# The last chunk's second product as three float32r products of split operands

## The chip, the cores and the metric

The kernel runs on one NeuronCore of a Trainium2 chip. A core has five engines, each with its own in-order program: TensorE (PE in the profile; its weight loads are listed as PEld), VectorE (DVE), ScalarE (ACT), GpSimd (POOL) and SyncE (SP, which here only issues DMAs). TensorE reads SBUF and writes to PSUM; the other engines work on SBUF and PSUM, GpSimd on SBUF alone. The engines wait for one another through semaphores. The metric is the device time of one execution in microseconds (us).

## The reference

All data are float32. A recurrent cell (mLSTM) runs over S = 768 steps for 4 batches and 8 heads of size 40; its output, reordered to x with 3072 rows (batch x step) and 320 columns, goes through two matrix products with a sigmoid-approximated GELU between them:

```python
    m_new = np.maximum(f_gate[:, :, t] + m, i_gate[:, :, t])
    f_stab = np.exp(f_gate[:, :, t] + m - m_new)
    i_stab = np.exp(i_gate[:, :, t] - m_new)
    m = m_new
    C = f_stab[:, :, None, None] * C + i_stab[:, :, None, None] * np.einsum('bhd,bhe->bhde', vt, kt)
    n = f_stab[:, :, None] * n + i_stab[:, :, None] * kt
    h_tilde = np.einsum('bhde,bhe->bhd', C, qt)
    nq = np.einsum('bhd,bhd->bh', n, qt)[:, :, None]
    denom = np.maximum(np.abs(nq), 1.0)
    o = 1.0 / (1.0 + np.exp(-o_gate[:, :, t]))
    y[:, :, t] = o * h_tilde / denom
...
    h = x @ w_in
    g = h * (1.0 / (1.0 + np.exp(-1.702 * h)))
    return (g @ w_out).astype(np.float32)
```

Here `w_in` is 320 x 2048 and `w_out` 2048 x 320. The change is in `g @ w_out`.

## The kernel before

The 768 steps are cut into six chunks of 128 (`NW` = 6, chunk number `w`). One chunk holds 128 steps of all four batches, so the two products have 512 rows of x in a chunk: four row blocks `b` of 128. The main loop (line 980) does for each chunk `w`: the first product and GELU of chunk `w`; then the second product of chunk `w`, cut into blocks, with the attention of chunk `w + 1` put between these blocks. The program order of every engine is the order in which the Python code issues its instructions; nothing is reordered (`manual_schedule`). So "behind" on an engine means later in the code.

**First product** (`up_fast`, line 789, from chunk 1 on). The 2048 hidden columns are 16 blocks of 128, worked on in eight pairs `j`. Each operand is split into a high part with 12 bits (`x_high`, `w_high`: a ScalarE copy to float32r with scale `BIAS`) and what remains; a pair is 16 float32r matmuls with 512 columns into two `main` and two `side` banks of PSUM. Then ScalarE takes the side banks times -4096 into the tile `g` (L823), VectorE adds main times (1 + 1/4096) to it (L825), and one pair later ScalarE applies the GELU in place (L784, `gelu_fast`). Even pairs take their banks from `banks()`, two tiles of two banks used in turn; odd pairs take single banks from the pool `ps_m`. So a pair uses the banks of the pair two before it.

**Second product, chunks 1 to 5** (`down_fast`, line 876). `w_out` stays in SBUF as `w_out_sb`, 16 blocks `f` of 128 rows by 320 columns. It is seen as four quarters, `w00`, `w01`, `w10`, `w11` (blocks 0-7 or 8-15, columns 0-159 or 160-319). Two row blocks at a time are multiplied with it by a seven-product scheme (Strassen-Winograd): seven products of 8 float32 matmuls with 160 columns (L889), on `g` or on sums of `g` (`s`), and on a quarter or on sums of quarters (`t1`, `t2`, `t4` in `t_sb`). The sums of weights are made once, in chunks 0 and 1, by GpSimd (L848); one of them, `weight_sums(2)`, overwrites `w01` with `w11 - w01` in chunk 1. The sums of `g` are made by GpSimd (`hidden_difference` L857, `hidden_sums` L865, L868) beside the pairs and by VectorE (L865, L868, `last_sums` L874) at their end. Each product is added from PSUM into an output tile by VectorE (L892, L894); a finished row block of 128 x 320 is stored by SP (L898). A chunk has 14 such blocks; list index `i` in the loop of line 1066.

**Between the blocks of chunk `w`** stands the attention of chunk `w + 1` (`attention`, line 967): exponentials on ScalarE, masks and decays on GpSimd, scores and values on TensorE, the output's scaling on VectorE. Its result goes to DRAM and back as squares (`seam_out` L587, `seam_in` L596), is transposed on VectorE (`seam_turn`, L603) and split (`split_x` L765, L766 on ScalarE; `split_on` L773, L775, L778 on VectorE) for the next chunk's first pair. SP also brings in `w_diff` and `w_low` from DRAM again for the next chunk (L754, L750), issued at `i` = 11 and 13.

**Chunk 0** takes its second product directly (`down`, L835: 320 columns in float32, 64 matmuls), and converts the weights on the way in.

SBUF tiles come from pools; a tile with the same tag in the same pool takes the room of an older one and waits until that one's last reader is done. The tiles that this change reuses are `v_st`, `k_st`, `k_sq`, `q_sq`, `t_sb`, `state0` and `state1` (inputs and states of the attention), the buffers of `kT`, `qT` and `wt` (attention), of `w_high` and `w_low` (tag `wb`) and of `w_diff` (pool `sp`, tag `g`).

Of the kernel before, what the change touches and what calls it, by code (L numbers as in the profile page):

```python
# [18 lines left out]
L = 128  # L19
# [12 lines left out]
def kernel(  # L32
# [44 lines left out]


    f_sb, i_sb = {}, {}
    k_st = const.tile([L, BH * D + DP - D], FP, name="k_st")  # L80
    q_sq = const.tile([L, BH // 2 * 4 * D + 32], FP, name="q_sq")
    k_sq = const.tile([L, BH // 2 * 4 * D + 32], FP, name="k_sq")
    t_sb = const.tile([128, 3, NH * DH], FP, name="t_sb")
# [4 lines left out]
    v_st = const.tile([L, BH, D1], FP, name="v_st")  # L88
# [4 lines left out]
    w_out_sb = const.tile([128, NF, DM], FP, name="w_out_sb")  # L93

    def load_gates(w):
        for dst, src in ((f_sb, f_gate), (i_sb, i_gate)):
# [43 lines left out]
    w_out_flat = w_out_sb.rearrange("p f m -> p (f m)")  # L140


    def piece_in(c, n):
# [7 lines left out]
    def piece_out(n):  # L151
        parts, c = [], n * 512
        while c < n * 512 + 512:
            f, m = divmod(c, DM)
            e = min(c + DM - m, n * 512 + 512)
            parts += [(slice(0, 128), slice(c - n * 512, e - n * 512), out_bits[:, f, 2 * m:2 * (m + e - c)])]
            c = e
        return w_out_flat[:, n * 512:(n + 1) * 512], parts

    pieces = []  # L160
    for n in range(4):
# [67 lines left out]
        G.memset(t[:, :, D:DP], 0.0)  # L229

    mark = const.tile([L, 1], FP, name="mark")
    state = [const.tile([128, BH // 2, D1], FP, name=f"state{i}") for i in range(2)]
    state_mid = const.tile([128, BH // 2, D1], FP, name="state_mid")

    m_at, ends = {0: m0}, {}
# [385 lines left out]
    def wait_for(x):  # L621

        G.tensor_copy(out=mark[0:x.shape[0]], in_=x[:, 0:1])
# [206 lines left out]
    def down(w, b, n):  # L830
        if n == 0:
            o_ps[w, b] = ps_m.tile([128, DM], FP, tag="m", name="p_out")
        po = o_ps[w, b]
        for f in range(n * 4, n * 4 + 4):
            T.matmul(po, gs[w, f // 2][:, f % 2, b * L:(b + 1) * L], w_out_sb[:, f, :], start=(f == 0),  # L835
                     stop=(f == NF - 1))
# [6 lines left out]
    w00, w01 = w_out_sb[:, 0:NH, 0:DH], w_out_sb[:, 0:NH, DH:DM]  # L843
    w10, w11 = w_out_sb[:, NH:NF, 0:DH], w_out_sb[:, NH:NF, DH:DM]

    def weight_sums(n):
        out, a, b = ((t1, w01, w00), (t2, w11, t1), (w01, w11, w01), (t4, w10, t2))[n]
# [28 lines left out]
    def down_fast(w, c):  # L876
# [19 lines left out]
        def store(two):  # L896
# [8 lines left out]
                lambda: (product(block(1, 1), t4, (o10, o10)), store(1)),  # L905
                lambda: (product(total(2), w11, (o01, o01)), store(0))]


    def run(calls):
        for f, *args in calls:  # L910
            f(*args)
# [68 lines left out]
    for w in range(NW):  # L980
        more = w + 1 < NW
        if w == 0:
            for j in range(NF // 2):
                if j % 2 == 0:
                    ahead, behind = converted[j // 2]
                    if j:
                        run([(convert, p) for p in ahead])
                    run([(fetch, p) for p in fetched.get(j // 2, ())])
                    up(w, j, lambda: run([(columns_turn, 1) if p is None else (convert, p) for p in behind]), last_seam)
                if j == 6:  # L990
                    load(1, "o")
                if j == 1:
                    wait_for(w_in[1][:, 1, :])
                    scale(0, 1)
                    load(1, "v")
                if j < B and j % 2:
                    carry(0, j // 2)
                if j == 3:
                    masks()
                    gates(1)  # L1000
                    columns_in(1)
                if j == 4:
                    spread(1)
                    load_squares(1, "q")
                if j >= B:
                    transposes(1, j - B)
        else:
            if w == 1:
                split_diff(1)
                split_low(1, V)  # L1010
                more_rooms(1)
            for j in range(NF // 2):
                up_fast(w, j)
                if more and j == 0:
                    gates(w + 1)
# [33 lines left out]
                lag = 3 if w == 1 else 2  # L1049
                if lag <= j < 4 + lag:  # L1050
                    hidden_difference(w, j - lag)
                if j >= 6:
                    hidden_sums(w, (j - 6,), G)
            gelu_fast(w, NF // 2 - 1)
            if more:
                load(w + 1, "o")
            hidden_sums(w, (2, 3), V)
        side = attention(w + 1) if more else {}
        if more:
            rooms(w + 1)  # L1060
        if w == 0:

            blocks = [(lambda b=b, n=n: down(w, b, n)) for n0 in (0, 2) for b in range(B) for n in (n0, n0 + 1)]
        else:
            blocks = down_fast(w, 0) + down_fast(w, 1)
        for i, block in enumerate(blocks):
            if w == 0 and i == 0:
                columns(1)
                convert_begin(17)
                weights_exp(1, 0)  # L1070
                fill_squares(q_sq)
                convert_end(17)
                for n in (1, 3, 5, 7):
                    block_transposes(1, n)
# [12 lines left out]
            if w == 0 and i == 5:  # L1087
                wait_for(w_out_flat[:, 9 * 512:])
                weight_sums(1)
                weight_sums(3)  # L1090
            if w == 0 and i == 5:
                split_high(0)
                split_rest()
                split_high(1)
            if w == 0 and i == 9:
                split_diff(0)
                split_low(0, V)
                split_rest_low()
            if w and more:
                if i == 11:  # L1100
# [38 lines left out]
```

## Time and profile before

| what | value |
|---|---|
| median of three runs | 446.97 us (446.6 to 446.97) |
| the profiled execution | 447.5 us, its span 445.8 us, 12211 instructions |
| eight pairs of chunk 5 (last) | 382.91 to 412.29 |
| second product of chunk 5 | 412.29 to 442.73 |
| TensorE clock granted | 1.00 in every stretch asked for |
| DMA, all queues | 60.06 MB, mean 135 GB/s |

How to read it: times inside the span count from its start. A group line gives line number, engine, operation, tiles written and read, shape and count, then busy time and mean duration in ns, then the engine's idle time before it and what ended it. A timeline line gives start, length, engine, line, operation and count, with the idle time before it in square brackets. A line of the chain gives start, length and what the end waited for there. TensorE overlaps its matmuls, so the mean duration of one is longer than the distance from one to the next; a float32 matmul is recorded as two instructions and a float32r one as one. The form shows f32 for float32r operands of a matmul. Stretches list busy time and count for PE, PEld, DVE, ACT and POOL, then the granted clock, the DMA share and GB/s.

### The profile page before, as it was taken

How to read it: one execution, taken by the hardware profiler on the slowest of the kernel's cores; microseconds unless marked ns; L12 is line 12 of the kernel's file. 1: busy time of each engine (PE TensorE's matmuls, PEld its weight loads, DVE VectorE, ACT ScalarE, POOL GpSimd, SP SyncE). 2: the span in 40 equal slices, each digit the busy share in tenths (PEclk: the TensorE clock that was granted, in tenths of full speed). 3: DMA queues.
4: the chain of work that ended last, by engine and by line, in shares of the span. 5: the costliest groups of instructions: out<-in, count | busy, mean ns of one | idle time of the engine just before them, and what ended most of it. 6: DMA issues, size and time to landing. Idle time of an engine off the chain costs nothing.

```text
span 445.8 us, 12211 instructions
## 1 busy us (share of the span) xinstructions
PE 440.1 (99%) x4999; PEld 384.0 (86%) x4999; DVE 327.3 (73%) x660; ACT 228.9 (51%) x494; POOL 130.8 (29%) x131
## 2 busy tenths in 40 slices
PE   8999999999999999999999999999999999999997
PEld 6867887776889999888999888999888999888997
DVE  4888999989999877778686779686769566634512
ACT  5677779902787701687701486800486900366000
POOL 6401327440066700135700034700035610035000
PEclk9999999999999999999999999999999999999999
DMA  8999999017777427979026978216988306600000
GB/s 168 196 283 165 242 271 216 2 35 196 183 200 161 63 63 218 267 111 168 13 59 188 270 102 176 44 34 143 328 114 156 61 19 151 232 31 0 1 31 29
DMA packets 129656, 60.06 MB, mean 135 GB/s; under 512 B 102096, under 2 KB 122528, under 8 KB 129600
## 3 DMA queue, kind: packets, MB, share of 16 engines
q1 hardware_dynamic: 120512, 54.86, 55.8%
q10 hardware_dynamic: 8768, 4.28, 3.3%
q8 instruction: 39, 0.64, 0.6%
q0 software_dynamic: 320, 0.15, 0.2%
q14 instruction: 17, 0.14, 0.1%
HBM read 49.10 MB, written 10.16 MB: 133 GB/s over the span
## 4 chain that ended last, share of the span: by engine, by line
PE 93%; SPq 4%; DMA 2%; DVE 1%; issue 0%; ACT 0%; DVEq 0%
PE p_out L889 34%; PE p L806 17%; PE p_h L806 16%; PE p_out L835 8%; PE p_h L657 7%; SPq L132 3%; PE p L534 2%; PE p L490 2%; PE p L542 2%; PE p L633 2%; PE p_h L666 2%; DMA bits<-in_moe_w_in_dram 2%; DVE state L610 0%; PE p L406 0%; DVE state_mid L642 0%
## 5 line engine op out<-in xcount | busy, mean ns | idle before, releaser
L857 POOL TENSOR_TENSOR g<-g 128x512 f32<-128x512 f32 x20 | 25.8, 1297 | 159.5 <-ACT g L784 159.5
L889 PE MATMUL p_out<-w_out_sb,g 128*128 128x160 f32 x480 | 68.9, 300 | 0.0
L889 PEld LDWEIGHTS p_out<-w_out_sb,g 128*128 128x128 f32 x480 | 66.4, 190 | 0.6
L765 ACT ACTIVATE x_high<-xT 128x512 fp32r<-128x512 f32 x10 | 6.3, 630 | 95.9 <-DVE xT L603 95.9
L894 DVE TENSOR_TENSOR o_sb<-o_sb,p_out 128x160 f32<-128x160 f32 x70 | 21.1, 318 | 44.8 <-PE p_out L889 44.7
L784 ACT ACTIVATE g<-g 128x512 f32<-128x512 f32 x80 | 46.4, 627 | 2.9 <-DVE g L825 2.6
L889 PE MATMUL p_out<-t_sb,s 128*128 128x160 f32 x320 | 47.1, 300 | 0.0
L825 DVE SCALAR_TENSOR_TENSOR g<-p,g 128x512 f32<-128x512 f32 x40 | 25.7, 681 | 27.3 <-PE p L806 12.8
L889 PEld LDWEIGHTS p_out<-t_sb,s 128*128 128x128 f32 x320 | 44.4, 190 | 0.2
L823 ACT ACTIVATE g<-p 128x512 f32<-128x512 f32 x40 | 21.7, 597 | 39.4 <-PE p L806 38.1
L463 ACT ACTIVATE wt<-wt,cols 128x64 f32<-128x64 f32 x160 | 38.9, 334 | 0.1
L835 PE MATMUL p_out<-w_out_sb,g 128*128 128x320 f32 x128 | 35.7, 436 | 0.0
L825 DVE SCALAR_TENSOR_TENSOR g<-p_h,g 128x512 f32<-128x512 f32 x40 | 26.4, 683 | 11.3 <-PE p_h L806 8.1
L835 PEld LDWEIGHTS p_out<-w_out_sb,g 128*128 128x128 f32 x128 | 23.9, 190 | 9.6
L657 PE MATMUL p_h<-xT,w_in 128*128 128x256 f32 x128 | 29.8, 385 | 1.1 <-ACT xT L574 1.1
L657 PEld LDWEIGHTS p_h<-xT,w_in 128*128 128x128 f32 x128 | 23.6, 190 | 6.4 <-issue 2.2
L823 ACT ACTIVATE g<-p_h 128x512 f32<-128x512 f32 x40 | 23.4, 595 | 10.2 <-PE p_h L806 10.2
L470 POOL TENSOR_SCALAR_AFFINE_SELECT wt<-wt 64x1024 f32<-64x1024 f32 x20 | 24.6, 1230 | 6.9 <-ACT wt L463 6.2
L806 PE MATMUL p_h<-x_diff,w_diff 128*128 128x512 f32 x80 | 25.1, 394 | 0.0
L806 PE MATMUL p<-x_rest,w_rest 128*128 128x512 f32 x80 | 25.1, 394 | 0.0
L806 PE MATMUL p_h<-x_rest,w_rest 128*128 128x512 f32 x80 | 25.0, 394 | 0.0
L806 PE MATMUL p<-x_diff,w_diff 128*128 128x512 f32 x80 | 25.0, 393 | 0.0
(206 smaller groups left out, 936.7 us busy)
## 6 DMA issues: line engine op xcount, KB each, us to landing
w_diff<-w_row SPq DMA_DIRECT2D x16, 512.0 KB, 4.8
wt<-m_row SPq DMA_DIRECT2D x20, 256.0 KB, 5.6
bits<-in_moe_w_in_dram SPq DMA_DIRECT2D x8, 512.0 KB, 10.0
out_dram<-o_sb SPq DMA_DIRECT2D x24, 160.0 KB, 3.1
q_sq<-in_q_dram SPq DMA_DIRECT2D x10, 320.0 KB, 8.6
eo<-in_o_gate_dram SPq DMA_DIRECT2D x5, 640.0 KB, 5.4
bits<-in_moe_w_out_dram SPq DMA_DIRECT2D x8, 320.0 KB, 5.7
q_sq<-x_row SPq DMA_DIRECT2D x10, 256.0 KB, 2.9
```

The lines of the kernel that those rows point to most:

```text
L132: nc.sync.dma_start(out=dst[:, hs, 0:D], in_=src[bs, :, w * L:(w + 1) * L, :].rearrange("b h s d -> s (b h) d"))
L463: A.activation(out=x[:, h, :], in_=x[:, h, :], func=AF.Exp, scale=-1.0, bias=cols[w][:, c * PH + h:c * PH + h + 1])
L470: G.affine_select(out=r, in_=r, compare_op=OP.is_ge, fill=0.0, base=0, pattern=[[0, PH], [1, HL]], channel_multiplier=-1)
L657: T.matmul(ph[j][i][:, t], w_in[f // 4][:, c, f % 4 * 128:f % 4 * 128 + 128], x[:, c, t], start=(first and c == 0 and n == 0), stop=(not f ...
L784: A.activation(out=g, in_=g, func=AF.Gelu_apprx_sigmoid)
L806: T.matmul(dst[i], a(i), x, start=(first and m == which[0]), stop=(last and m == which[-1]))
L823: A.activation(out=g[:, i, :], in_=side[i], func=AF.Copy, scale=-BASE)
L825: V.scalar_tensor_tensor(out=g[:, i, :], in0=main[i], scalar=1.0 + 1.0 / BASE, in1=g[:, i, :], op0=OP.mult, op1=OP.add)
L835: T.matmul(po, gs[w, f // 2][:, f % 2, b * L:(b + 1) * L], w_out_sb[:, f, :], start=(f == 0), stop=(f == NF - 1))
L857: G.tensor_tensor(out=a10, in0=a00, in1=a10, op=OP.subtract)
L889: T.matmul(po, a(f), b[:, f, :], start=(f == 0), stop=(f == NH - 1))
L894: V.tensor_tensor(out=dst, in0=x, in1=po, op=OP.add)
```

## The change

The last chunk (`w` = 5) no longer uses the seven-product scheme. Each of its four row blocks is multiplied with the whole of `w_out` by three float32r products, in two PSUM banks: high x high and low x low into `main`, diff x diff into `side`. For an operand x the parts are `h`, a float32r copy with scale 1 - 2^-13 (ScalarE), `d = x - (1 + 1/4096) h` and `l`. For `g`, `l = x - h`; for the weights, `l = 4096 d + h`. A row block takes 16 x 3 matmuls of 320 columns. ScalarE then writes -4096 x `side` to the output tile, VectorE adds (1 + 1/4096) x `main`, SP stores it.

What is issued where:

- The weight parts (`out_part`) need 3 x 16 x 320 columns. They are put into rooms that are free by then. Two high parts of 1280 columns are made by ScalarE after block 8 of chunk 4; two diffs by VectorE ahead of the eight pairs of chunk 5; the others beside pairs 0 to 6, one part of 1280 columns in one or two instructions on VectorE a pair, and on ScalarE two halves beside each of pairs 2 and 3.
- The parts of `g` (`g_split`) for row block 0 are made one pair behind the pairs: `h` on ScalarE, `d` on VectorE, `l` on GpSimd. Those of row blocks 1, 2, 3 are made by ScalarE and twice VectorE: block 1 after the pairs, blocks 2 and 3 behind the join of blocks 0 and 1.
- Since `w01` is overwritten in chunk 1, GpSimd stores it to DRAM first (`keep_w01`, 640 KB) and loads it again after block 13 of chunk 4 (`fetch_w01`).
- `w_out_sb` becomes two tiles of eight blocks each, so that the second one's room can be used again.
- `hidden_difference` and `hidden_sums` go in chunk 5.

Chunks 1 to 4 keep the seven products. The diff, cut to its core:

```diff
+    w_out_sb = [const.tile([128, NH, DM], FP, tag=f"w_out{i}", name=f"w_out{i}") for i in range(2)]
...
+    pairs_out = (4, 5, 6, 0, 1, 2, 3, 7)
+    def keep_w01():
+        w01_row.append(rows.tile([128, NH, DH], FP, tag="w01", bufs=1, name="w01_row"))
+        G.dma_start(out=w01_row[0], in_=w01)
+    def fetch_w01():
+        G.dma_start(out=w01, in_=w01_row[0])
+    def out_part(part, f, n=4):
...
+        if part == 0:
+            A.activation(out=to, in_=w, func=AF.Copy, scale=BIAS)
+        elif part == 1:
+            V.scalar_tensor_tensor(out=to, in0=h.bitcast(FP), scalar=-1.0 - 1.0 / BASE, in1=w, op0=OP.mult, op1=OP.add)
+        else:
+            d, at = wo[1, f]
+            V.scalar_tensor_tensor(out=to, in0=d[:, at:at + n].bitcast(FP), scalar=BASE, in1=h.bitcast(FP), op0=OP.mult,
+                                   op1=OP.add)
+    def g_split(j, b, engine):
...
+        h, d, low = (g_part[n, b, j] for n in range(3))
+        x = gs[NW - 1, j][:, :, b * L:(b + 1) * L]
+        A.activation(out=h, in_=x, func=AF.Copy, scale=BIAS)
+        V.scalar_tensor_tensor(out=d, in0=h.bitcast(FP), scalar=-1.0 - 1.0 / BASE, in1=x, op0=OP.mult, op1=OP.add)
+        engine.tensor_tensor(out=low, in0=x, in1=h.bitcast(FP), op=OP.subtract)
+    def down_parts(b):
+        both = banks("p_out")
+        main, side = both[:, 0, 0:DM], both[:, 1, 0:DM]
+        order = [f for j in pairs_out for f in (2 * j, 2 * j + 1)]
+        for f in order:
+            for n, dst in enumerate((main, side, main)):
+                T.matmul(dst, g_part[n, b, f // 2][:, f % 2], wo[n, f][0][:, wo[n, f][1]],
+                         start=(f == order[0] and n < 2), stop=(f == order[-1] and n > 0))
+        o = op.tile([128, DM], FP, tag="o", name="o_sb")
+        A.activation(out=o, in_=side, func=AF.Copy, scale=-BASE)
+        V.scalar_tensor_tensor(out=o, in0=main, scalar=1.0 + 1.0 / BASE, in1=o, op0=OP.mult, op1=OP.add)
+        t = (NW - 1) * L
+        nc.sync.dma_start(out=out[b * S + t:b * S + t + L, :], in_=o)
...
+            if not more:
+                room_out(1, 8, 4, "v_st", 1312)
+                room_out(1, 12, 4, "k_st", 1304)
+                out_part(1, 8)
+                out_part(1, 12)
...
                     if j == 0:
                         split_high(2)
+                        keep_w01()
...
+                if not more:
...
+                    run([(out_part, *x) for x in (((2, 8),), ((2, 12),), ((0, 0, 2), (0, 2, 2)),
+                                                  ((0, 4, 2), (0, 6, 2), (1, 0)), ((1, 4),), ((2, 0),),
+                                                  ((2, 4, 2), (2, 6, 2)), ())[j]])
+                    if j:
+                        g_split(j - 1, 0, G)
+                    continue
...
-            hidden_sums(w, (2, 3), V)
+            if more:
+                hidden_sums(w, (2, 3), V)
+            else:
+                g_split(NF // 2 - 1, 0, G)
+                for j in pairs_out:
+                    g_split(j, 1, V)
...
-            blocks = down_fast(w, 0) + down_fast(w, 1)
+            blocks = []
+            for b in range(B):
+                down_parts(b)
+                if b + 2 < B:
+                    for j in pairs_out:
+                        g_split(j, b + 2, V)
...
+                if w + 2 == NW and i == 8:
+                    room_out(0, 8, 8, "k_sq", 2592)
+                    out_part(0, 8)
+                    out_part(0, 12)
                 if i == 13:
                     fetch_diff(w + 1, (2, 3))
+                    if w + 2 == NW:
+                        fetch_w01()
```

More of the change, by code (lines that the diff above doesn't have):

```diff
@@ L79 @@
     f_sb, i_sb = {}, {}
[L80 to L83, printed above, removed]
+    k_st = const.tile([L, BH * D + DP - D], FP, tag="k_st", name="k_st")
+    q_sq = const.tile([L, BH // 2 * 4 * D + 32], FP, tag="q_sq", name="q_sq")
+    k_sq = const.tile([L, BH // 2 * 4 * D + 32], FP, tag="k_sq", name="k_sq")
+    t_sb = const.tile([128, 3, NH * DH], FP, tag="t_sb", name="t_sb")
     t1, t2, t4 = (t_sb[:, i, :].rearrange("p (f m) -> p f m", m=DH) for i in range(3))
@@ L87 @@
     at_bits, at_const = BH * DP, BH * DP + 1024
-    v_st = const.tile([L, BH, D1], FP, name="v_st")
+    v_st = const.tile([L, BH, D1], FP, tag="v_st", name="v_st")
     eo = {}
@@ L92 @@
     w_in_x = work.tile([128, NF // 2, 128], FP, tag="xh", bufs=1, name="w_in_x")
-    w_out_sb = const.tile([128, NF, DM], FP, name="w_out_sb")
+    w_out_sb = [const.tile([128, NH, DM], FP, tag=f"w_out{i}", name=f"w_out{i}") for i in range(2)]
     def load_gates(w):
@@ L138 @@
     out_bits = w_out_bits.rearrange("(f p) m -> p f m", p=128)
-    w_out_flat = w_out_sb.rearrange("p f m -> p (f m)")
+    w_out_flat = [x.rearrange("p f m -> p (f m)") for x in w_out_sb]
     def piece_in(c, n):
@@ L157, in piece_out @@
             c = e
-        return w_out_flat[:, n * 512:(n + 1) * 512], parts
+        return w_out_flat[n // 5][:, n % 5 * 512:(n % 5 + 1) * 512], parts
     pieces = []
@@ L231 @@
     mark = const.tile([L, 1], FP, name="mark")
-    state = [const.tile([128, BH // 2, D1], FP, name=f"state{i}") for i in range(2)]
+    state = [const.tile([128, BH // 2, D1], FP, tag=f"state{i}", name=f"state{i}") for i in range(2)]
     state_mid = const.tile([128, BH // 2, D1], FP, name="state_mid")
@@ L834, in down @@
         for f in range(n * 4, n * 4 + 4):
-            T.matmul(po, gs[w, f // 2][:, f % 2, b * L:(b + 1) * L], w_out_sb[:, f, :], start=(f == 0),
+            T.matmul(po, gs[w, f // 2][:, f % 2, b * L:(b + 1) * L], w_out_sb[f // NH][:, f % NH, :], start=(f == 0),
                      stop=(f == NF - 1))
@@ L840, in down @@
             nc.sync.dma_start(out=out[b * S + w * L:b * S + (w + 1) * L, :], in_=o)
-    w00, w01 = w_out_sb[:, 0:NH, 0:DH], w_out_sb[:, 0:NH, DH:DM]
-    w10, w11 = w_out_sb[:, NH:NF, 0:DH], w_out_sb[:, NH:NF, DH:DM]
+    (w00, w01), (w10, w11) = ((x[:, :, 0:DH], x[:, :, DH:DM]) for x in w_out_sb)
     def weight_sums(n):
@@ L906, in down_fast, with room_out @@
                 lambda: (product(total(2), w11, (o01, o01)), store(0))]
+    w01_row = []
+    pairs_out = (4, 5, 6, 0, 1, 2, 3, 7)
+    wo, g_part = {}, {}
+    def keep_w01():
[3 more added lines that the diff above has]
+        G.dma_start(out=w01, in_=w01_row[0])
+    def room_out(part, f, nf, tag, n):
+        t = const.tile([128, n], FR, tag=tag, name="w_part")
+        t = t[:, 0:nf * DM].rearrange("p (f m) -> p f m", m=DM)
+        wo.update({(part, f + x): (t, x) for x in range(nf)})
@@ new lines, in out_part @@
+    def out_part(part, f, n=4):
+        (h, at), (to, x) = wo[0, f], wo[part, f]
+        h, to, w = h[:, at:at + n], to[:, x:x + n], w_out_sb[f // NH][:, f % NH:f % NH + n]
+        if part == 0:
[6 more added lines that the diff above has]
+                                   op1=OP.add)
@@ new lines, in g_split @@
+    def g_split(j, b, engine):
+        if b % 2 == 0 and (0, b, 0) not in g_part:
+            for part, name in ((0, "kT"), (1, "qT")):
+                for n in range(4):
+                    t = work.tile([128, 2, 2, L], FR, tag=name, bufs=4, name=name)
+                    g_part.update({(part, b, 2 * n + x): t[:, x] for x in range(2)})
+        if (2, b, j) not in g_part:
+            j0 = j // 4 * 4
+            for part in range(3) if b % 2 else (2,):
+                if part == 2:
+                    pool, tag, n = (win, "wb", 3) if b % 2 else (work, "wt", 2)
+                    t = pool.tile([128, 4, 2, L], FR, tag=tag, bufs=n, name="g_part")
+                else:
+                    t = sp.tile([128, 4, 2, L], FR, tag="g", name="g_part")
+                g_part.update({(part, b, j0 + x): t[:, x] for x in range(4)})
+        h, d, low = (g_part[n, b, j] for n in range(3))
[3 more added lines that the diff above has]
+        engine.tensor_tensor(out=low, in0=x, in1=h.bitcast(FP), op=OP.subtract)
@@ L1049 @@
                 lag = 3 if w == 1 else 2
+                if not more:
+                    if j == 0:
+                        room_out(2, 8, 12, "t_sb", 3840)
+                        wo.update({(2, f): (wo[2, 8][0], 8 + f) for f in range(4)})
+                    if j == 2:
+                        room_out(0, 0, 8, "w_out1", 2560)
+                    if j == 3:
+                        room_out(1, 0, 8, "q_sq", 2592)
+                    if j == 6:
+                        room_out(2, 4, 2, "state0", 656)
+                        room_out(2, 6, 2, "state1", 656)
+                    run([(out_part, *x) for x in (((2, 8),), ((2, 12),), ((0, 0, 2), (0, 2, 2)),
[4 more added lines that the diff above has]
+                    continue
                 if lag <= j < 4 + lag:
@@ L1056 @@
                 load(w + 1, "o")
-            hidden_sums(w, (2, 3), V)
+            if more:
+                hidden_sums(w, (2, 3), V)
+            else:
+                g_split(NF // 2 - 1, 0, G)
+                for j in pairs_out:
+                    g_split(j, 1, V)
         side = attention(w + 1) if more else {}
@@ L1063 @@
             blocks = [(lambda b=b, n=n: down(w, b, n)) for n0 in (0, 2) for b in range(B) for n in (n0, n0 + 1)]
-        else:
-            blocks = down_fast(w, 0) + down_fast(w, 1)
+        elif more:
+            blocks = down_fast(w, 0) + down_fast(w, 1)
+        else:
+            blocks = []
[4 more added lines that the diff above has]
+                        g_split(j, b + 2, V)
         for i, block in enumerate(blocks):
@@ L1087 @@
             if w == 0 and i == 5:
-                wait_for(w_out_flat[:, 9 * 512:])
+                wait_for(w_out_flat[1][:, 4 * 512:])
                 weight_sums(1)
```

## The prediction

> **What bounds the kernel now.** I read the page's busy shares first, then the chain that ended last, then the last 63 us more closely: that chain, the groups by shape, stretches and single rows. TensorE is busy for 99% of the span, so another engine's time counts only where TensorE waits for it.
>
> ```profile
> PE 440.1 (99%) x4999; PEld 384.0 (86%) x4999; DVE 327.3 (73%) x660; ACT 228.9 (51%) x494; POOL 130.8 (29%) x131
> ```
>
> The chain of the last chunk, start and length in us. Eight first-product pairs of 3.67 us stand in a row with nothing between them; then the second product takes 30.44 us, and after it only one VectorE add and the last store (443.08 to 445.8).
>
> ```profile
> 379.92 2.99 PE p_out L889 x22
> 382.91 3.67 PE p L806 x16
> ...
> 408.62 3.67 PE p_h L806 x16
> 412.29 30.44 PE p_out L889 x224
> 442.73 0.02 issue
> 442.76 0.32 DVE o_sb L894
> ```
>
> The two stretches by engine: the first pairs have free time on all engines but TensorE; the second product leaves ACT and POOL almost idle.
>
> ```profile
> 382.91:412.29 29.38, 29.38 (x130) 24.03 (x130) 11.95 (x21) 17.78 (x32) 10.35 (x8) 1.00 0.16 55
> 412.29:442.73 30.44, 30.43 (x225) 30.19 (x223) 10.42 (x28) 1.18 (x2) 0.00 (x0) 1.00 0.05 17
> ```
>
> Groups of these stretches (busy us, mean ns of one). A float32r matmul on 512 columns (L806) and a float32 one on 160 (L889), each with its weight load: the float32 loads overlap one another (13.1 us for 95 of 190 ns), the float32r ones do not (3.0 us for 16 of 188 ns).
>
> ```profile
> L889 PEld LDWEIGHTS p_out<-w_out_sb,g 128*128 128x128 f32 x95 | 13.1, 190 | 0.0
> L806 PEld LDWEIGHTS p<-x_diff,w_diff 128*128 128x128 f32 x16 | 3.0, 188 | 0.7
> ```
>
> Single rows used below: VectorE's pair of two-input operations beside a working GpSimd and without one, ScalarE's long gap before the last chunk, GpSimd's, and DMA issues (median us to landing).
>
> ```profile
> 351.10 1.07 DVE L874 TENSOR_TENSOR s<-g,s 128x256 f32<-128x256 f32 x2
> ...
> 419.09 0.75 DVE L874 TENSOR_TENSOR s<-g,s 128x256 f32<-128x256 f32 x2
> ```
> ```profile
> 378.04 0.63 ACT L765 ACTIVATE x_high<-xT 128x512 fp32r<-128x512 f32 x1 [21.36 <-DVE xT L603]
> ```
> ```profile
> 391.67 1.29 POOL L857 TENSOR_TENSOR g<-g 128x512 f32<-128x512 f32 x1 [33.73 <-ACT g L784]
> ```
> ```profile
> raw<-st_row SPq DMA_DIRECT2D x16, 12.0 KB, 3.0
> ...
> raw<-st_row POOLq DMA_DIRECT2D x4, 12.0 KB, 6.5
> ```
>
> **The change, part by part.**
>
> *Second product on TensorE.* Out go 14 blocks of 8 float32 products, recorded as 224 instructions: 30.44/224 = 135.9 ns each. In come 4 x 16 x 3 = 192 float32r matmuls of 320 columns, which the trace does not have. float32 costs 135.9/160 = 0.85 ns a column; float32r on 512 costs 3.67/16 = 229.4 ns. At half the float32 rate, 512 columns would be 217.4, so 12.0 ns come on top. If nothing comes on top at 320 columns: 135.9 ns, 26.1 us. If the surcharge goes by columns: 229.4 x 320/512 = 143.4 ns, 27.5 us. If it goes by instruction: 147.9 ns, 28.4 us. I take the middle of the last two, both being extrapolations of the same row: 145.7 ns, 28.0 us. Gain 2.4 us, ends 2.0 and 4.3. The Trainium skill (TensorE: Matmul & The Clock Gate, Back-to-back issue gap) gives N/2.4 + 2.5 ns for an isolated warm matmul, which would be 136 ns and 26.1 us; by the same formula 512 columns would take 216, and this trace has 229.4, so the row decides.
>
> *The end.* Now: the add (0.32). Then: ScalarE takes the side bank (a 128x320 copy at L839 took 0.42), starting one matmul, 0.15, before the end, and VectorE joins both banks (128x320 at L509: 0.49), with some 0.1 for two hand-overs: 0.85. That is 0.5 us more. The last store is unchanged.
>
> *Splits of the first rows of g, and weight parts, beside the eight pairs.* VectorE has 1.29 us a pair now. A weight part of 1280 columns: L775 takes 691 ns for 512 and L720 1216 for 1024, so 1.48; a split of 256 columns 0.42 (L773). Sum 3.2 of 3.67 us: hidden. Two parts stand ahead of pair 0: VectorE is free at 384.9, so it reaches that pair's L825 at 387.85 instead of 387.31; the banks are wanted again at 390.25 or later, so nothing waits. ScalarE: 1.1 + 1.15 now, and 0.40 for a split: 2.7; in pairs 2 and 3 also 1.5 for weight parts (1254 ns for 1280 columns at L394, in halves): 4.2, so it is 1.1 us late after both and makes it up in two pairs. A bank comes back two pairs (7.3 us) later. GpSimd does 0.7 a pair (half of L857's 1.29) instead of 1.29 or 2.6. Cost zero; if that cover goes, each us that VectorE is late at pair 7 can become a wait of the second product.
>
> *Hand-over.* The second product asks for pairs in the order 4, 5, 6, 0, 1, 2, 3, 7. Pair 6 is wanted at 412.3 + 12 x 0.146 = 414.05; ScalarE splits it after its GELU, about 412.6, VectorE and GpSimd follow by 413.3. Margin 0.75 us, the thinnest here. Pair 7 is wanted at 418.4 and ready by 414.7.
>
> *Splits for rows 1 to 3.* VectorE does two 256-column operations a pair, 0.75 (the row at 419.09), 6.0 for a row block, and the 0.49 join: 6.5 against TensorE's 48 x 0.146 = 7.0. It begins about 413.6 and TensorE needs the first of row 1 at 419.3, so it stays 4 to 6 us ahead, though each join in its queue waits for TensorE's end of that block and holds up the splits behind it. It would be late only above (439.4 - 413.6 - 1.0)/24 = 1.03 us a pair. ScalarE needs 8 x 0.40 + 0.42 = 3.6. Cost zero.
>
> *Two weight parts on ScalarE in chunk 4* (block 8): 2.5 us after its DMA issues end at 373.4, inside the 21.36 us gap, done by 375.9. Zero.
>
> *GpSimd's two DMAs* (640 KB each). The store comes behind the two L848, which end at 94.6, when DMA is 42% busy (96 to 100); the load behind the third product of chunk 4's second half, about 376.2. GpSimd itself has nothing to do until 126 and 391, so its issue, 0.55 us for small ones and unknown for these, is free. What they can cost is the transfers they meet. At 352 GB/s (380 to 382) 640 KB take 1.9 us. The load meets w_diff, issued at 377.54 and landed 3.6 later, 381.1, first used at 383.9: 2.8 of slack, more than 1.9. The store meets the x_row round trip of chunk 1, whose last transpose already waits 0.28 us for it. I take zero for both, since most of the store falls ahead of that round trip's second half; the ends are 0 and 1.9 each. Nothing gains.
>
> *What goes* (L857, L865, L868, L874, L892, L894 of the last chunk) ran beside TensorE: no gain.
>
> **Sum.** -2.4 + 0.5 = -1.9 us. The profiled execution took 447.5 (span 445.8), so it would be 445.6; it stands 0.5 over the median of 446.97, so the median becomes 445.1. This kernel's runs lie within 0.1%, and 0.2%, 0.9 us, is about what can be told from no change.
>
> **Rivals.**
>
> *The weight load bounds (slower).* In the rows float32r loads never overlap, because at 229 ns they need not. If they cannot, each matmul takes 188 ns: 36.1 us, 5.7 + 0.5 over before, 453.2. It decides from (30.44 - 0.5)/192 = 156 ns on. Against it: float32 loads of 190 ns are followed at 135.9 ns. The Trainium skill (TensorE: Matmul & The Clock Gate, Part 3, The mechanism) says that loads overlap matmuls in flight only for another row group; with its 107 ns a load that would be 243 ns and 46.6 us, but the trace disagrees, as 135.9 ns holds load and matmul. Chance 0.08.
>
> *VectorE blocked by GpSimd.* A two-input VectorE pair took 1.07 beside GpSimd and 0.75 without. Each pair now has GpSimd's 0.7 next to VectorE's weight part and split. If all of it is added, 3.9 against 3.67: 0.23 x 7 = 1.6 us late at pair 7, 0.75 of it covered, and a further late split may double the rest. 0.9 to 1.8 us: 446.0 to 446.9. The Trainium skill (SBUF — State Buffer, Who interferes with whom) has it that such an operation and a GpSimd one shut each other out for a whole instruction; by that rule it is this case. Chance 0.12, half of it still faster by 0.2%.
>
> *The DMAs collide.* 1 to 3.8 us of TensorE idle at the start of chunk 1 or 5: 446.1 to 448.9. For it: a queue of GpSimd took 6.5 us to land what SP's landed in 3.0. Against: the slack of 2.8. Chance 0.08.
>
> *No gain on TensorE*: reads beside busy ScalarE and VectorE push the pitch to 151 to 156 ns: 446.1 to 447.0. Chance 0.06.
>
> **Chances and range.** Forecast 0.66 (its own range 443.1, from 135.9 ns, to 445.6, from 147.9), load 0.08, blocked 0.12, DMAs 0.08, no gain 0.06. Faster by over 0.2%: 0.66 + 0.06 = 0.72. Within: half of blocked, most of no gain, a little of the DMAs: 0.12. Slower: 0.08, most of the DMAs, the rest: 0.16. The range, 443.1 to 447.8, leaves out the load and the worse DMA cases.
>
> **What would show it.** Right: 192 matmuls of 320 columns at 143 to 148 ns in one unbroken stretch of about 28 us from 412.3, pairs still of 3.67, a join of 0.4 to 0.5 on ScalarE and VectorE at the end. Wrong: a pitch over 150; TensorE waiting for a split of pair 6 or 7 or of a later row; a pair longer than 3.67; L806 of chunk 1 or 5 starting late behind a DMA.

## The result, and the profile after

The changed kernel takes 448.61 us (median of 22 runs, 444.67 to 451.47), beside 446.70 for the kernel before (22 runs, 445.62 to 447.57). The ratio is 1.0041, 95% interval 1.0023 to 1.0059: slower by some 1.8 us, where 1.9 us faster was predicted. One of the 22, the 451.47, is in a slower state and is left out of the ratio. The profiled execution took 449.82 us, its span 448.1 us.

The last chunk did what was predicted. The loss lies 300 us ahead of it, at the start of chunk 1, where GpSimd's store of `w01` delays another transfer. (After the change the lines of the old kernel from 843 to 898 have numbers smaller by one; L963, L966 and L967 are the new product and its join, L914 and L917 the store and the load.)

The chain of the last chunk after the change, start and length in us, and the two stretches (PE, PEld, DVE, ACT, POOL, granted clock, DMA share, GB/s):

```profile
386.83 3.67 PE p L806 x16
...
412.54 3.68 PE p_h L806 x16
416.22 28.19 PE p L963 x192
444.42 0.02 issue
444.44 0.45 ACT o_sb L966
444.88 0.02 issue
444.91 0.49 DVE o_sb L967
```
```profile
386.83:416.22 29.39, 29.39 (x130) 24.03 (x130) 25.63 (x36) 22.38 (x42) 5.85 (x6) 1.00 0.21 77
416.22:444.41 28.19, 28.18 (x193) 27.92 (x191) 19.85 (x55) 10.63 (x31) 1.72 (x2) 1.00 0.05 19
```

28.19 us stand where 30.44 stood; eight pairs of 3.67 to 3.68 still stand ahead of them with nothing between, though VectorE is now busy for 25.63 of their 29.39 us (before 11.95) and ScalarE for 22.38 (17.78). TensorE never waits for a split.

The start of chunk 1 is another matter. First the chain before, then after:

```profile
96.28 13.12 PE p_out L835 x48
109.40 0.01 issue
109.41 3.99 PE p L806 x16
```
```profile
95.68 4.62 DMA x_row<-y
...
101.95 5.35 DMA x_rest<-y
...
107.99 2.38 DMA q_sq<-x_rest
...
110.72 0.61 DVE xT L603
...
111.35 0.64 ACT x_high L765
111.99 0.04 issue
112.03 5.33 PE p L806 x16
```

Before, TensorE's own work leads into the first pair. After, the chain runs through the round trip of x by DRAM, and TensorE waits for it. The list of TensorE's waits puts the price beside it (us in total, times, longest):

```profile
PE p L806 <- ACT x_high L765: 3.3, 1, 3.3
```

Why the round trip is late can be read from the issues and the landings. GpSimd's issue, after; then SP's, before and after; then the times from issue to landing (last number, us), before and after:

```profile
93.85 0.88 POOL L914 DMA_DIRECT2D w_row<-w_out  x1
```
```profile
96.36 0.94 SPq L587 DMA_DIRECT2D x_row<-y  x2
...
99.06 0.36 SPq L596 DMA_DIRECT2D q_sq<-x_row  x1
```
```profile
95.68 1.70 SPq L587 DMA_DIRECT2D x_row<-y  x2
...
100.74 0.36 SPq L596 DMA_DIRECT2D q_sq<-x_row  x1
```
```profile
x_row<-y SPq DMA_DIRECT2D x2, 128.0 KB, 2.1
...
x_rest<-y ACTq DMA_DIRECT2D x2, 32.0 KB, 3.1
```
```profile
x_row<-y SPq DMA_DIRECT2D x2, 128.0 KB, 4.6
...
x_rest<-y ACTq DMA_DIRECT2D x2, 32.0 KB, 5.4
```

SP issued `x_row` 0.7 us earlier than before, but could read it back only 1.7 us later: from issue to read-back 5.1 us instead of 2.7. Counting the packets in the trace: the store's are 4480 bytes, 264 ns each, nine tenths of them from 95.3 to 97.5 us and the last at 99.1. Until 97.6 not one packet of `x_row` (256 bytes, 19 ns) ran, and its 1024 packets then took until 100.2; before, they ran from 97.3 to 98.6. SP's late read-back then fell on the second half of the round trip, which ScalarE's queue issues at 100.4 as before (100.31). The read-back's packets (`q_sq<-x_row`) ran from 101.9 to 103.3, amid the `x_row` packets of the second half; before, they ran from 100.1 to 101.5, ahead of most of them. The `x_rest` behind took 5.4 us from issue to landing instead of 3.1. That the one made the other late is read from this order in time; no run tests this link by itself.

The wait costs more than its length. Single microseconds of the first pair (the granted clock is third from the end):

```profile
112.00:113.00 1.00, 0.96 (x2) 0.83 (x3) 0.95 (x2) 0.93 (x3) 0.00 (x0) 0.50 1.19 211
113.00:114.00 1.00, 1.00 (x4) 0.75 (x3) 0.97 (x4) 0.00 (x0) 0.00 (x0) 0.50 1.13 205
114.00:115.00 1.00, 1.00 (x4) 0.81 (x3) 1.00 (x3) 0.00 (x0) 0.00 (x0) 0.50 0.75 175
115.00:116.00 1.00, 1.00 (x5) 0.83 (x5) 1.00 (x2) 0.00 (x0) 0.00 (x0) 0.96 1.11 266
```

After TensorE's idle 3.3 us the clock was at half for some 3.4 us, and the pair took 5.33 us instead of 3.99. So in the profiled executions: chunk 1 begins 2.62 later (112.03 against 109.41), the way from there to chunk 5 takes 1.30 longer (386.83 - 112.03 = 274.80 against 273.50), the rest 1.62 less (448.1 - 386.83 = 61.27 against 62.89): together the +2.3 between the spans.

How often the clock dropped can be read from the mean granted clock, which is on record for each execution: one stretch of 3.4 us at half clock in 448 lowers it to 0.996. Of the changed kernel's 21 executions in the ratio, 14 stand at 0.996 or less, with a median of 449.5 us, and seven at 0.999 or more, with a median of 446.99, about level with before. So the loss in the median comes with the executions in which the clock dropped; where it didn't, the changed kernel is only level with before.

### The profile page after: what moved, and what is told of

Same layout as the page of the kernel before. It is cut to its first block, busy times and chain, and to the rows that moved or that the text cites. A ratio compares the mean times of both kernels' runs of the same rounds, so it can differ in the third digit from the quotient of the medians.

```text
span 448.1 us, 12222 instructions
## 1 busy us (share of the span) xinstructions
PE 439.0 (98%) x4967; PEld 382.8 (85%) x4967; DVE 351.1 (78%) x701; ACT 245.8 (55%) x536; POOL 130.5 (29%) x133
## 4 chain that ended last, share of the span: by engine, by line
PE 90%; DVE 4%; DMA 3%; POOL 1%; issue 1%; ACT 0%; ACTq 0%; SPq 0%; DVEq 0%; POOLq 0%
PE p_out L888 28%; PE p L806 17%; PE p_h L806 16%; PE p_h L657 6%; PE p L963 6%; PE p L534 2%; PE p_out L835 2%; PE p L542 2%; PE p L490 2%; PE p L633 2%; PE p_h L666 2%; PE p L406 1%; DMA x_rest<-y 1%; DMA x_row<-y 1%; PE p_o L524 1%; PE p_s L479 1%
## 5 line engine op out<-in xcount | busy, mean ns | idle before, releaser
L856 POOL TENSOR_TENSOR g<-g 128x512 f32<-128x512 f32 x16 | 20.6, 1296 | 119.5 <-ACT g L784 119.5
L888 PE MATMUL p_out<-w_out,g 128*128 128x160 f32 x384 | 55.2, 300 | 0.0
L888 PEld LDWEIGHTS p_out<-w_out,g 128*128 128x128 f32 x384 | 53.1, 190 | 0.5
L893 DVE TENSOR_TENSOR o_sb<-o_sb,p_out 128x160 f32<-128x160 f32 x56 | 16.8, 317 | 27.0 <-PE p_out L888 26.9
L888 PE MATMUL p_out<-t_sb,s 128*128 128x160 f32 x256 | 37.8, 301 | 0.0
L888 PEld LDWEIGHTS p_out<-t_sb,s 128*128 128x128 f32 x256 | 35.5, 190 | 0.2
L835 PE MATMUL p_out<-w_out,g 128*128 128x320 f32 x128 | 35.7, 436 | 0.0
L835 PEld LDWEIGHTS p_out<-w_out,g 128*128 128x128 f32 x128 | 23.9, 190 | 9.6
L806 PE MATMUL p<-x_high,w_high 128*128 128x512 f32 x80 | 25.3, 409 | 3.3 <-ACT x_high L765 3.3
```

Of the source, the lines that this page charges most:

```text
L806: T.matmul(dst[i], a(i), x, start=(first and m == which[0]), stop=(last and m == which[-1]))
L856: G.tensor_tensor(out=a10, in0=a00, in1=a10, op=OP.subtract)
L888: T.matmul(po, a(f), b[:, f, :], start=(f == 0), stop=(f == NH - 1))
L893: V.tensor_tensor(out=dst, in0=x, in1=po, op=OP.add)
```

## The experiments

My first theory was that the store costs the start of chunk 1 and the load nothing; the rivals, that the weight load or VectorE had eaten the gain (the profile already denied both), or that only the lower clock matters. All kernels but e2 start from the changed one; all compute the whole output. One table holds the profiled executions in three stretches (us): up to chunk 1's first pair, from there to chunk 5's, and the rest. Each row is one execution, while the ratio is that of all; e4, e5 and e8 are told in the text.

| kernel | to chunk 1 | to chunk 5 | rest | ratio to before, interval |
|---|---|---|---|---|
| before | 109.41 | 273.50 | 62.89 | 1 |
| changed | 112.03 | 274.80 | 61.27 | 1.0041, 1.0023 to 1.0059 |
| e1 store late | 109.38 | 272.86 | 61.26 | 1.0005, 0.9984 to 1.0026 |
| e2 before + store | 111.74 | 275.02 | 62.84 | 1.0092, 1.0056 to 1.0128 |
| e3 store early, GpSimd | 109.97 | 274.93 | 61.60 | 1.0053, 1.0033 to 1.0073 |
| e6 no store, no load | 109.50 | 273.41 | 61.29 | 0.9938, 0.9907 to 0.9969 |
| e7 store and load late | 108.47 | 273.25 | 61.28 | 0.9909, 0.9873 to 0.9945 |
| e9 load late | 111.58 | 273.20 | 61.32 | 1.0042, 1.0011 to 1.0073 |
| e10 store late, ScalarE | 107.86 | 273.59 | 61.75 | 1.0001, 0.9973 to 1.0029 |
| e11 = e7 | 108.66 | 273.09 | 61.25 | 0.9965, 0.9935 to 0.9995 |
| e12 store early, ScalarE | 107.48 | 273.43 | 61.89 | 0.9997, 0.9969 to 1.0024 |

**e1_store_after_split**: GpSimd waits for the last split of chunk 1's x before it stores.

```diff
+                        wait_for(x_rest[1][1].bitcast(FP)[:, W // 2:])
                         keep_w01()
```

> The changed kernel, with GpSimd waiting for the last split of chunk 1's x (its x_rest, about 112.6 us) before it stores the quarter w01. Theory A (the store's 640 KB stand in the way of chunk 1's x_row round trip, and what they cost is TensorE's wait and the slow clock after it): chunk 1's first pair starts at about 109 as before and takes 3.99, the second product stays at 28.2, total about 445.1 (444.7 to 445.6), faster than before by 0.3 to 0.4%. Theory B (the loss at chunk 1 comes from elsewhere: another layout of the tiles, other instruction fetches): about 448.6 still. Rival within A: the store now meets the DMAs of chunk 1's own pairs, and a pair is longer than 3.67.

446.49 us (444.62 to 449.48), against 446.4. In the profiled execution TensorE does not wait for `x_high` at all, the clock is 1.00 throughout, and the first pairs still take 3.67. So the store's place makes the wait at chunk 1. But the median is only level with before, where 1.9 us less were due: something still costs.

**e2_store_alone**: the kernel before, with the store at its new place and nothing else; the stored row is read by nobody.

```diff
+    def keep_w01():
+        w01_row.append(rows.tile([128, NH, DH], FP, tag="w01", bufs=1, name="w01_row"))
+        G.dma_start(out=w01_row[0], in_=w01)
...
                         split_high(2)
+                        keep_w01()
```

> The kernel before, with the store of w01 to DRAM alone, at the same place as in the change; nothing reads it back. Theory A: chunk 1's first pair starts 2 to 3.3 us late and, where TensorE has idled so long, runs 1.3 us slower; total 448.5 to 451, and as widely spread from run to run as the changed kernel. Theory B: 446.7, as before.

451.17 us against 446.4; by the ratio, 4.1 us slower. The store alone costs more than the changed kernel as a whole loses. Part of this is the clock: five of its eight executions have a mean clock of 0.996 or less, three of them 0.992, which is two stretches; the other three have a median of 448.57, 2.2 above before. Its chain has the same late piece, and the same slow pair:

```profile
102.06 5.03 DMA x_rest<-y
...
107.78 2.30 DMA q_sq<-x_rest
...
111.74 5.54 PE p L806 x16
```

**e3_store_before_sums**: the store ahead of GpSimd's two sums of weights, some 6 us earlier.

```diff
                 wait_for(w_out_flat[1][:, 4 * 512:])
+                keep_w01()
                 weight_sums(1)
                 weight_sums(3)
```

> The changed kernel, with the store of w01 put ahead of GpSimd's two weight sums instead of behind them: its transfer runs at about 89 to 92 us, when the DMA engines are idle, and is over before x_row is issued. Theory A: as with the late store, about 445.1 (444.7 to 445.6), and chunk 1's first pair starts 0 to 1 us later than before at most. Rival C (GpSimd's DMA costs where it stands because GpSimd is held up by it, not by its bytes): the weight sums end later by a us or more and the total is over 446.

448.34 us, not the 445.1 of theory A. The store's packets now ran from 90 to 92.5 us, in a pause of all other transfers, and chunk 1 waits only 0.2. GpSimd's sums end 1.4 us later, as rival C has it (95.3 against 93.9), but chunk 1 begins only 0.6 later than before. But in this execution chunk 5 waits 1.2, and its chain passes through the transfers that the load meets:

```profile
373.56 3.53 DMA x_rest<-y
...
377.77 5.46 DMA q_sq<-x_rest
...
384.22 0.64 ACT x_high L765
384.86 0.04 issue
384.90 3.98 PE p L806 x16
```

While the load's 4480-byte packets run (379 to 382.2 us), the 512-byte packets of `q_sq<-x_rest` come at 20 to 35 in half a microsecond instead of some 124. The same collision, then, at the other end, and my theory that the load is free is in doubt.

**e4_filler**: 100 tiny matmuls ahead of chunk 1's first pair, to keep TensorE busy during the wait and tell the price of the clock from that of the wait.

```diff
-        if j == 0 and w in (2, 3):
+        if j == 0 and w in (1, 2, 3):
...
-            for _ in range(10):
+            for _ in range(100 if w == 1 else 10):
```

> The changed kernel, with 100 tiny matmuls (8x8, 26 ns each, 2.6 us) on TensorE ahead of chunk 1's first pair, which is when it idles; their results are overwritten. Theory A in two parts: if 1.3 us of the loss is the clock of 0.50 after the idle time, the pair takes 4.0 instead of 5.3 and the total is about 447.5; the wait for x_high itself stays. If the pair is long because VectorE's splits come late, nothing is gained: 448.6 or a little more, where the fillers stand in the way.

In the profiled execution the first pair took 3.76 us instead of 5.33: the clock held. But the kernel took 451.72 us (450.5 to 455.81) instead of the 447.5 expected, and in the profiled execution a new wait arose later:

```profile
112.22 3.76 PE p L806 x16
...
123.50 10.93 DMA v_st<-in_v_dram
...
136.83 5.52 PE p L806 x16
```

ScalarE stood behind the issue of a late `w_row<-w_diff` (132.91 us; in the changed kernel 128.69), TensorE waited 2.5 us for it, and that pair ran at half clock. (Another such stretch began at 25.03, far ahead of the filler.) Whether the filler kept the clock at chunk 1 isn't shown: in e8 and e9 below the pair kept it in the profiled execution without a filler. Why the transfers of chunk 1 came later isn't shown either.

**e5_half_columns**: each matmul of the product cut into two of 160 columns, to see what the weight load allows.

```diff
-                T.matmul(dst, g_part[n, b, f // 2][:, f % 2], wo[n, f][0][:, wo[n, f][1]],
+                for s in (slice(0, DH), slice(DH, DM)):
+                    T.matmul(dst[:, s], g_part[n, b, f // 2][:, f % 2], wo[n, f][0][:, wo[n, f][1]][:, s],
```

> The changed kernel with each float32r matmul of the last product cut in two of 160 columns, so 384 of them. At 320 columns the distance is 146.8 ns, at 512 it is 227 in steady work: both are the columns at 2.4 per ns plus 13.3 ns. If those 13.3 ns are a fixed part of each matmul and the weight load stays hidden: 66.7 + 13.3 = 80 ns, 30.7 us for the product. If the weight load sets the pace (188 ns long, never seen overlapping in float32r before the change): at least 107 to 146 ns, 41 to 56 us. If the surcharge goes by columns: 71 to 73 ns, 28 us.

One execution: 463.8 us. The chain's piece, and a group of the loads (mean ns of one last but one):

```profile
415.54 42.86 PE p L964 x384
```
```profile
L964 PEld LDWEIGHTS p<-w_part,g_part 128*128 128x128 f32 x256 | 31.2, 192 | 0.0
```

42.86/384 = 111.6 ns from one matmul to the next. Half of the 146.8 ns that 320 columns took would be 73.4, so something else than the columns sets the pace here; what, isn't shown. Each matmul has one load before it, so loads of 192 ns each overlap and can follow one another at 111.6 ns. That is below 146.8, so the load doesn't bound the product at 320 columns, and "the weight load bounds" is out.

**e6_rebuild**: no store and no load; GpSimd rebuilds `w01` from `w11` and the difference, at the old place of the load.

```diff
-        G.dma_start(out=w01, in_=w01_row[0])
+        for n in range(0, NH, 2):
+            G.tensor_tensor(out=w01[:, n:n + 2], in0=w11[:, n:n + 2], in1=w01[:, n:n + 2], op=OP.subtract)
...
-                        keep_w01()
```

> The changed kernel without store and load: GpSimd rebuilds w01 as w11 - (w11 - w01) in four pieces of 0.75 us behind the last reader in chunk 4 (about 376), which rounds once more. Theory A (all of the loss is the two transfers): 446.5 - 1.6 = 444.9, spread as the kernel before (2 to 3 us), chunk 1 and chunk 5 begin as before. Theory B: 448.6. Rival within A: the pieces hold up VectorE's two-input operations at 376 to 380 (each by up to 0.75) and chunk 5's first pair starts up to 1 us late: 445 to 446.

445.65 us (444.54 to 446.47), against 447.26 on that chip: without the two DMAs the change is a gain. In the profiled execution chunk 1's first pair still waits 0.7 us for `x_high`, so not all of such a wait needs the store.

**e7_both_late** and, on another chip, **e11_both_late_again**: the store as in e1, the load behind the last split of chunk 5's x.

```diff
             if not more:
...
+                wait_for(x_rest[w][1].bitcast(FP)[:, W // 2:])
+                fetch_w01()
...
-                    if w + 2 == NW:
-                        fetch_w01()
```

> The changed kernel with both transfers moved out of the round trips: the store behind chunk 1's last split of x, the load behind chunk 5's (about 384.5, wanted by ScalarE at about 391). Theory A, with the load as the cause of what the kernel with the late store alone still lost (446.5, up to 449.5): 444.9, spread as before. If the load was harmless: 446.5 again. If the load now comes too late: ScalarE's weight parts beside pair 2 wait, and the second product starts late.

> The kernel of e7 once more, beside the two above on one chip. If e7's gain is real and not that chip's: ratio 0.992 to 0.996 (the profiled execution before is 447.5, less the 1.9 us worked out for TensorE and the end: 0.9957; e7 had 0.9909 against a before that spread to 451.9). If e7 was luck: within 0.002 of 1.

444.55 us (443.83 to 445.9) against 447.26, and 445.22 (443.21 to 449.84) against 447.03: faster than both kernels, about 445, what had been forecast. By the medians the ratios are 0.994 and 0.996. e7's 0.9909 lies 0.3% below that; on its chip before spread widely, as five of its 20 executions took over 450 us, at a mean clock of 0.996 or less. In e7 the round trip is quick again, and GpSimd issues both DMAs once each first pair is under way:

```profile
101.00 2.46 DMA x_rest<-y
...
108.47 3.99 PE p L806 x16
```
```profile
112.78 0.89 POOL L914 DMA_DIRECT2D w_row<-w_out  x1
```
```profile
383.88 0.95 POOL L917 DMA_DIRECT2D w_out<-w_row  x1 [0.30 <-issue]
```

**e8_short_runs**: the row in DRAM laid out so that the store's pieces would be 640 bytes long, to tell the size of packets from their number.

```diff
-        w01_row.append(rows.tile([128, NH, DH], FP, tag="w01", bufs=1, name="w01_row"))
+        w01_row.append(rows.tile([NH, 128, DH], FP, tag="w01", bufs=1, name="w01_row"))
```

> The changed kernel, store and load at their old places and of the same size, but with the quarter laid out in DRAM so that each run is 640 bytes instead of 5120 (the packets were 4480 and 640 bytes). If the DMA engines take turns packet by packet between queues, a small packet of the round trip waits some 40 ns for each instead of 173 to 264, and the loss shrinks by more than half: 445 to 446.5. If bytes alone count: 448.6 as before, or worse, as short packets move fewer bytes in a us.

449.66 us, ratio 1.0040 (1.0005 to 1.0074), and the same wait of 3.3 us, though the clock held in the profiled execution. But the packets were still of 4480 bytes: GpSimd's queue joined seven pieces of 640. The premise wasn't met, and nothing follows on the size.

**e9_load_late**: only the load moved, as in e7.

> The changed kernel with only the load moved (behind the last split of chunk 5's x, as in e7); the store stays ahead of chunk 1. If the store's meeting with x_row and x_rest is the main loss and the load's a smaller one (e3 showed 1.5 us of waiting at chunk 5, e1 a kernel level with before): chunk 1's first pair late by 2 to 3 us again and at half the clock, chunk 5 without a wait, and a median 1 to 2 us under the changed kernel's 448.6: ratio 0.999 to 1.002. If the load costs nothing: 448 to 449, ratio 1.003 to 1.005. If the load is the main loss: 445 or less, ratio under 0.997.

449.03 us against 447.03: no better than the changed kernel. The wait at chunk 1 is there:

```profile
PE p L806 <- ACT x_high L765: 2.6, 1, 2.6
```

This time the pair behind it ran at full clock (3.99).

**e10_store_by_act** and **e12_store_by_act_early**: the store by ScalarE's queue, behind block 11 (e10, shown) or block 7 (e12, with `i == 7`) of chunk 0.

```diff
-        G.dma_start(out=w01_row[0], in_=w01)
+        nc.scalar.dma_start(out=w01_row[0], in_=w01)
...
+            if w == 0 and i == 11:
+                keep_w01()
             if w == 0 and i == 9:
```

> The changed kernel with the store issued by ScalarE's queue behind block 11 of chunk 0 (about 94 us, where GpSimd issued it), same bytes, same moment. If it is the bytes that cost, x_row lands late here too, some 1.9 us of transfer at 350 GB/s, and chunk 1 starts 2 to 3 us late as in the changed kernel. If it is GpSimd's queue (its packets of 4480 bytes, or its late and long issue), then packets of 640 bytes by ScalarE's queue share the engines with x_row's 512-byte ones, x_row lands within 3 us of its issue, chunk 1's first pair waits under 1 us, and the kernel is near e1's ratio of 1.0005 or below.

> As e10, but the store stands behind block 7 of chunk 0, whose copy ends at 94.0 us in the changed kernel, so that ScalarE's queue issues it at the moment at which GpSimd issued it (93.85); in e10 it went out only at 105.4, behind the x_row and x_rest round trip. If the bytes cost, whatever the queue: x_row's first half lands more than 4 us after its issue, chunk 1's first pair waits 2 to 3 us, and the ratio is 1.003 to 1.005 as in the changed kernel. If it is GpSimd's queue: 640-byte packets beside x_row's, the first half lands within 3 us, the wait is under 1 us, ratio 0.998 to 1.001 as in e1 and e10. Rival of its own: ScalarE's half of x_row stands behind the store in ScalarE's queue and lands late instead, with the same wait of 2 us or more.

446.29 us against 447.03, and 446.61 against 446.64. Neither issued at the moment meant: ScalarE reached the store at 105.4 us in e10 (behind the round trip) and already at 84.7 in e12 (all its 640-byte packets ran between 85 and 89, with no other data moving). So they tell nothing of GpSimd's queue against another at the same moment; that stays open. They do show, with e1, that a store that runs before or behind the round trip costs chunk 1 at most 0.24 us of waiting, by either queue.

**What is settled, and what isn't.** The store at its place costs a wait of 2.2 to 3.3 us in the changed kernel, in e2, e5, e8 and e9, and at most 0.24 in e1, e3, e7, e10, e11 and e12: that is shown. (e6, with no store, has 0.7.) The steps that lead to it go the same way: with the store at its place SP's issue of the two `x_row` takes 1.70 to 1.75 us, they land in 3.8 to 4.6 us, and ScalarE's `x_rest` in 4.2 to 5.6; in the other kernels, before included, it is 0.94 to 1.05, 2.1, and 2.5 to 3.1. The price of the load isn't settled. With a harmless store and the old load the ratio is 1.0005, 1.0001 and 0.9997; with the load late too 0.9909 and 0.9965, which makes the load worth 0.3 to 1%, the upper end resting on e7, whose ratio lies below that of its medians. But with the harmful store, moving the load gained nothing (e9), and 4.1 us for the store alone (e2) less 1.6 is already more than the changed kernel loses. The clock explains part of e2's excess, not this: in e1, e10 and e12 eleven of twelve executions have a mean clock of 0.998 or more. The profiles don't help: those of e1, e10 and e12 hold no wait at chunk 5, and were quicker than their medians (e12's took 444.58, median 446.61), so what the other executions lose isn't seen. Only e3's shows the load's collision.

## Why the prediction was right or wrong, step by step

*Second product on TensorE*: right. 28.0 us were taken and 28.19 measured: 28.19/192 = 146.8 ns a matmul, between the 143.4 of "by column" and the 147.9 of "by instruction", near the latter: over the 135.9 of 320 columns without a surcharge 10.9 come on top, at 512 columns 12.0. The rival *the weight load bounds* is answered here too: the float32r loads, 188 ns each, follow one another at 146.8 ns, so they do overlap, and e5 had them at 111.6.

*The end*: 0.5 us taken; 0.6 came (448.1 - 444.41 = 3.7 us behind the last matmul, against 445.8 - 442.73 = 3.1). Product and end make -1.6 where -1.9 was summed.

*Splits and weight parts beside the pairs*, *hand-over* and *rows 1 to 3*: the verdicts were right; no pair grew and the product is unbroken. The thinnest place was that named, pair 6: VectorE was done with it at 417.63, wanted at 417.98, 0.35 of margin instead of 0.75. VectorE came to this split only at 417.03, behind weight parts of 1.65 to 1.73 us instead of the 1.48 worked out, and the split itself took 0.60 instead of 0.42. So *VectorE blocked by GpSimd* is there, but costs nothing. A weight part took longer only where GpSimd was already at work when it began; where GpSimd began inside one (396.05, the part running from 395.35 for 1.48), its operation took 1.72 instead of 0.74. The parts lost 0.17 to 0.25 us, less than the 0.29 to 0.38 that was left of GpSimd's operation, where the rival had added all of it.

*GpSimd's two DMAs*: wrong, and this is the step that failed: "I take zero for both, since most of the store falls ahead of that round trip's second half". It does, but it falls on the first half, which SP issued 1.8 us behind the store. The first half landed late, its read-back was pushed onto the second half, and so the second half was late without ever meeting the store. The bound of 1.9 us was too low too: 640 KB were counted at 352 GB/s, but nine tenths of the store's packets took 2.2 us and the rest until 99.1, and `x_row` landed 2.5 us later after its issue than before. And the bound left out what a wait does to the clock: 1.34 us on the pair here. For the load the zero is not shown wrong in the changed kernel's profile, where chunk 5 waits for nothing; e3 shows 1.2 us.

The evidence was in the trace of before. The last transpose already waited 0.28 us for this round trip, so whatever holds up its last transfer reaches ScalarE's split of x behind it:

```profile
108.73 0.63 ACT L765 ACTIVATE x_high<-xT 128x512 fp32r<-128x512 f32 x1 [0.93 <-DVE xT L603]
```

This row of before ends at 109.36, and TensorE's first pair begins at 109.41: 0.05 us of slack in all. *The DMAs collide* had the right mechanism and place, with 446.1 to 448.9 as its times and a chance of 0.08; 448.61 fell at its upper end, in part by luck, as the rival priced the idle time alone and not the clock. A chain with 0.05 us of slack and a transfer of unknown rate in its way deserved far more.

## What to carry to other kernels

Before adding a transfer, look for every round trip whose reader already waits, and follow both its halves: an early piece that is late pushes its read-back onto the next piece. Place the new transfer by a wait on the reader of that round trip (e7), not where its data happen to be ready; here this turned a loss of 0.4% into a gain of 0.35 to 0.9% by the ratios, 0.4 to 0.6% by the medians. And price an idle TensorE above its length, as the clock may drop behind it.

## What the runs showed of the hardware

The clock. An idle TensorE of 3.34 us (changed kernel), 2.18 (e2) and 2.20 (e5) was followed by half clock; idle times of 3.27 (e8) and 2.55 (e9) were not. These are the profiled executions; of all 12 of e8, ten have a mean clock of 0.996 or less, and nine of e9's, so one and the same kernel drops or keeps it. In e4 an idle time of 1.33 us, ending at 24.56, was followed by half clock from 25.03, and in before one of 1.05 at the same place wasn't. So the length doesn't decide alone. The time at half clock was the same: in the changed kernel from 111.67 to 115.09, in e2 from 112.93 to 116.34, 3.41 us each, and in e2 it began 1.2 us after TensorE was at work again. By the clock's own records it began 102.40 us, or 30 times 3.413, after the clock's first rise, in the changed kernel, e2 and e5 alike, and in e4 20.48 us, or 6 times, after it. The Trainium skill (TensorE: Matmul & The Clock Gate, What's actually happening) tells of a free-running window of 3413 ns over which the activity is judged; the trace agrees with that length and with a phase that doesn't follow the work, but not with the section's need of a whole idle window, since 2.2 us were enough, and in e4 1.3. Which share of a window must be idle, these traces don't settle.

Small packets beside large ones. The Trainium skill (DMA: Bandwidth & Descriptors, Queues, rings and completion order) says that each DMA engine takes its queues in turn, one whole packet at a time. The trickle in e3 agrees with this: taken in turn, a 512-byte packet of 27 ns and one of 264 ns make 27 of each in half a microsecond on 16 engines, and from 380 to 381.5 us the trace has 20 to 35 small ones and 29 to 34 large ones. Up to 97.6 us of the changed kernel even that trickle is missing, and SP's issue of the two `x_row` DMAs itself took 1.70 us instead of 0.94; what held them isn't shown.
